# Idle products, halved first weights and row scaling at the hand-over from attention to the first expert

## The chip, the cores and the metric

The kernel runs on one core of a Trainium2 chip. The metric is the device time of one execution in microseconds (us). An engine executes its own instructions in the order in which they were issued to it, and instructions of different engines wait for one another through semaphores. TensorE (PE in the profile; its weight loads are PEld), VectorE (DVE), ScalarE (ACT), GpSimd (POOL) and SyncE (SP, which only issues DMAs here) all take part. The clock of TensorE can be throttled; the profile records the share that was granted.

## The reference

The reference is an attention followed by a mixture of experts whose tokens are assigned by capacity:

```python
scores = scale * np.matmul(q, k.transpose(0, 1, 3, 2))     # q, k, v: 8 x 8 x 576 x 64
thresh = np.max(scores, axis=-1, keepdims=True) - tau
scores = np.where(scores >= thresh, scores, -1000000000.0)
attn = np.exp(scores - np.max(scores, axis=-1, keepdims=True))
attn = attn / (np.sum(attn, axis=-1, keepdims=True) + 1e-09)
x = rows of attn @ v                                       # 4608 x 512
logits = x @ w_gate                                        # 8 experts
order = np.argsort(-logits.flatten())
# walk down the order: a token takes the first expert that still has room, 576 tokens each
for e in range(8):
    out[assigned == e] = np.maximum(x[assigned == e] @ w1[e], 0.0) @ w2[e]
```

w1 is 8 x 512 x 1024, w2 is 8 x 1024 x 512, all in float32.

## The kernel before, in words

**Attention** (`attention`, lines 23 to 356) takes 32 pairs of heads in turn. At its end the last batches are transposed back to rows: `xt_unit` (line 204) does four transposes into PSUM (line 208), two copies on ScalarE (line 218) and a DMA into the DRAM table `xrows` (line 219). A row there has 512 values that are not yet normalised and 8 factors, one for each head. These units stand in the list `late` and are issued between the steps of the first expert search (lines 351 to 355).

**Router.** The experts are filled one after the other. `Router.phase` (line 598) finds an expert's threshold by a search of seven steps: a comparison on VectorE (`step_cmp`), a count by matmuls (`step_cnt`, line 463), a flag (`step_flag`, line 469, whose result `jka` VectorE reads from PSUM), and sums (`step_n`, lines 485 to 499). `pick` names the expert, `rank1` and `rank2` (lines 541 and 542) give each of its tokens a place, and `pack` (line 632) turns the places into a list `idx` of 576 rows: a one-hot compare, matmuls (line 568), a gather by matmuls (line 575) and `compact2`. The first search runs while attention ends (`alone`); the search of expert r+1 runs while expert r is computed. All of them write small results into one PSUM bank: in attention a slot of `sc`, later the single tile `rps`. `warm(n)` (line 594) issues n products of two constant matrices into other columns of that bank; nothing reads them. `pack` of the first expert calls it three times, with 20, 4 and 50 (`WARM`, line 650).

**Experts** (`moe`, line 653). For each expert r:

- `w1_load` (line 675) reads the number of the expert and loads w1 in four tiles `w1s` of 128 x 1024, for expert 0 from ScalarE's queue. Each float32 matrix is split into a rounded high part (`w1h`, a copy on ScalarE) and a low part (`w1l`, a subtraction on VectorE), so that a product is done as three: high x high, high x low, low x high. For expert 0 the four high parts are issued first, then the low parts in column blocks 0, 1, 2 to 3 and 4 to 7, each behind a certain point of `rows`.
- `w2_load` (line 706) does the same for w2 (`w2s`, `w2h`, `w2l`), loaded from SP's queue once GpSimd has copied the number of the expert behind its gathers. The splitting starts once all of w1 is split.
- `rows` (line 723) gathers the 576 rows in five tiles `xg` (four of 128, one of 64) by indirect DMAs from GpSimd (line 729). A tile is scaled by its factors (`scale` on VectorE, or `scale_act`, eight copies of 64 columns on ScalarE, line 739), transposed (`turn`, line 755), copied as the high part `xh` (line 756) and subtracted for the low part `xl` (`low`).
- `ffn` (line 784) does the products. The first layer (line 810) goes over eight blocks f of 128 columns of w1 and two halves of the rows; expert 0 does the first half of the rows (columns 0 to 255) for blocks 0 and 1 first. A block's result passes through ScalarE (relu and the high part of `H`), and VectorE makes the low part of `H`. The second layer (line 842) takes five tiles of rows, with w2 in eight parts.

**What sets the order.** The program is issued in an order that a clock written by hand decides: `clk` counts time, each job is a generator that yields how long its next step should come later, and `ffn` advances the clock by a stated cost for each product (0.25 for a half block of expert 0, 0.132 otherwise, 0.227 in the second layer; line 811, 843). `V.wait()` and `V.ease()` are estimates of when VectorE will be free. A job may wait for a name in the set `done`: `("w1",0)`, `("half",0)`, `("row",0,t)`, `("x",0)`, `"ahead"`. Low parts that can wait are put into `fills` and issued in the gaps of a search, when VectorE is thought free, when they are old, or when `ffn` wants them (`want`). For expert 0, `rows` also issues the start of expert 1's search by hand: `phase` up to its first comparison behind the gathers (lines 740 to 742), then the count and the flag at line 767; the rest runs once `"ahead"` is set. The products start to be issued once `("w1",0)` and `("half",0)` are there. The clock decides the order in each engine's queue, not when an instruction runs.

Of the kernel before, what the change touches and what calls it, by code (L numbers as in the profile page):

```python
# [398 lines left out]
class Router:  # L399
# [198 lines left out]
    def phase(s,last=False):  # L598

        s.stage="search"; V=s.V  # L600
        def held(t): s.pe=t; V.after(V.now+t+0.2)
        if s.first: s.prep(33)
        else:
            yield V.ease()
            s.prep()
            yield V.ease()
        s.alone=s.first; s.first=False
        if last:

            lo=s.wk.tile([128,1],F32,name="lo"); V.memset(lo,-FMAX/4); E={"lo":lo}  # L610
        else:
            E={"E":s.k("E1"),"lv":-1}
            def gap():

                w=V.wait(); s.fill()
                return w
            s.on=True
            for i in range(7):
                s.step_cmp(E); yield gap()
                held(0.34); s.step_cnt(); yield gap()  # L620
                held(0.16); s.step_flag(E["lv"]); yield gap()
                held(0.1); E=s.step_n(E)
                if not s.alone: yield V.ease()
            s.on=False
        s.pick(E)
        if last:
            yield V.wait()
            held(0.13); s.pick2()
        s.stage="pick"; s.rank1(E)
        yield V.wait()  # L630
        held(0.2); s.rank2()
# [16 lines left out]

LATS=[0.15,0.35,0.7]+[0.8]*5; FIX=(0.125,0.15)
GA=[5.0,6.5,8.0,8.0]; AGE=7.0; HALF=1; WARM=[20,4,50]  # L650
W1Y=5.0; L2O=(0,4,1,2,3); L2Z=1; HFB=3; RW=[0.2,0.4,0.4,0.4]; LOWP=(); LPF=7; LOWT=1.4; PREPW=1; WLY=(1.0,1.0)

def moe(ctx,tc,R,start,xrows,w1,w2,out,ident):
    nc=tc.nc
# [20 lines left out]
    def w1_load(r,s):  # L675
# [2 lines left out]
        s["e"]=q.value_load(s["ei"][0:1,0:1],min_val=0,max_val=E-1)  # L678
        for k in range(4):
            t=w1p.tile([128,F],F32,name="w1s",bufs=4); s["w1s",k]=t  # L680
            q.dma_start(t,w1[ds(s["e"],1),k*128:(k+1)*128,:].rearrange("o p f -> p (o f)"))
        yield W1Y if r==0 else 5.0
        while r>0 and ("l1",r-1) not in done: yield 0.5
        s["w1h"]=w1p.tile([128,4,F],F32R,name="w1h"); s["w1l"]=w1p.tile([128,4,F],F32R,name="w1l")
        if r==0:
            for k in range(4):
                A.activation(s["w1h"][:,k],s["w1s",k],AF.Copy); yield 1.1
            done.add(("w1",0))
            for a,b in ((0,1),(1,2),(2,4),(4,8)):
                while (("row",0,1),"scaled",("row",0,4))[min(a,2)] not in done: yield 0.1  # L690
                o=slice(128*a,128*b)
                for k in range(4):
                    V.tensor_tensor(s["w1l"][:,k,o],s["w1s",k][:,o],s["w1h"][:,k,o].bitcast(F32),op=ALU.subtract)
                    if a>1: yield 0.9 if a<4 else 2.0
                for f in range(a,b): done.add(("w1l",f))
            done.add(("w1a",0))
            return
        def lowpart(k,o): V.tensor_tensor(s["w1l"][:,k,o],s["w1s",k][:,o],s["w1h"][:,k,o].bitcast(F32),op=ALU.subtract)
# [7 lines left out]
    def w2_load(r,s):  # L706
        while ("g",r) not in done or (r>0 and ("w2",r-1) not in done): yield 0.5
        e=nc.sync.value_load(s["ei2"][0:1,0:1],min_val=0,max_val=E-1)
        for k in range(4):
            t=wk.tile([128,2,D],F32,name="w2s",bufs=4); s["w2s",k]=t  # L710
            nc.sync.dma_start(t,w2[ds(e,1),k*256:(k+1)*256,:].rearrange("o (k p) d -> p (o k) d",p=128))
        yield 5.0
        while ("w1a",r) not in done or (r==0 and ("x",0) not in done) or (r>0 and ("l2",r-1) not in done): yield 0.5
        s["w2h"]=wk.tile([128,8,D],F32R,name="w2h"); s["w2l"]=wk.tile([128,8,D],F32R,name="w2l")
        def lowpart(k,c): V.tensor_tensor(s["w2l"][:,2*k+c],s["w2s",k][:,c],s["w2h"][:,2*k+c].bitcast(F32),op=ALU.subtract)
        for k in range(4):
            for c in range(2):
                A.activation(s["w2h"][:,2*k+c],s["w2s",k][:,c],AF.Copy)
                yield WLY[0]
                later(("w2l",r,2*k+c) if 2*k+c<7 else ("w2",r),lambda k=k,c=c: lowpart(k,c))  # L720
                yield WLY[1]

    def rows(r,s):
# [8 lines left out]
        def scale(t):  # L732
# [1 line left out]
            n=128 if t<4 else 64  # L734
            v=s["xg",t][:n,:D].rearrange("p (h d) -> p h d",h=8)
            V.tensor_tensor(v,v,s["xg",t][:n,D:XW].unsqueeze(2).to_broadcast([n,8,64]),op=ALU.mult)
        def scale_act(t):
            x=s["xg",t]
            for h in range(8): A.activation(x[:,64*h:64*h+64],x[:,64*h:64*h+64],AF.Copy,scale=x[:,D+h:D+h+1])
        if r==0:  # L740
            step0=R.phase(); R.ahead=step0
            for _ in range(3): next(step0)
        yield GA[min(r,3)]
        while r>0 and ("l1",r-1) not in done: yield 0.5
        s["xh"]=wk.tile([128,4,576],F32R,name="xh"); s["xl"]=wk.tile([128,4,576],F32R,name="xl")
# [16 lines left out]
        if r==0:  # L762


            def step(n=1):
                for _ in range(n): next(R.ahead)
            step(); scale(0); step(); turn(0); scale(1); low(0); turn(1); scale_act(2); yield V.ease()
            low(1); yield 0.25
            scale(3); scale(4); done.add("scaled"); yield 1.8
            turn(2); yield 0.6  # L770
            turn(3); low(2); yield 0.6
            turn(4); low(3); yield 0.6
            low(4); done.add("ahead")
            done.add(("x",0)); return
        scale(order[0]); yield V.wait()
        for i,t in enumerate(order):
# [203 lines left out]
```

## Time and profile before

| | us |
|---|---|
| median of the timed runs (3) | 994.23 |
| lowest and highest of them | 993.36 and 996.37 |
| profiled execution, its own time | 986.18 |
| span of its instructions | 984.40 |
| PE busy | 952.5 |
| DVE busy | 780.3 |
| ACT busy | 633.9 |
| POOL busy | 261.0 |
| mean granted TensorE clock | 0.99 |

The span runs from the first to the last instruction of the profiled execution. A row of a timeline has the start, the length, the engine, the line, the operation, the tile that is written and the tiles that are read, how often (x), and in brackets the idle time of the engine before it with what ended it. Many VectorE instructions have line 395, since a helper issues them; the tiles tell them apart. Ends of PE instructions are modelled, and matmuls overlap. Attention takes the first 460 us, the first search lies between 465 and 486 us, expert 0 starts near 500 us, and the seven others follow, the second at 570 us.

### The profile page before, as it was taken

How to read it: one execution, taken by the hardware profiler on the slowest of the kernel's cores; microseconds unless marked ns; L12 is line 12 of the kernel's file. 1: busy time of each engine (PE TensorE's matmuls, PEld its weight loads, DVE VectorE, ACT ScalarE, POOL GpSimd, SP SyncE). 2: the span in 40 equal slices, each digit the busy share in tenths (PEclk: the TensorE clock that was granted, in tenths of full speed). 3: DMA queues.
4: the chain of work that ended last, by engine and by line, in shares of the span. 5: the costliest groups of instructions: out<-in, count | busy, mean ns of one | idle time of the engine just before them, and what ended most of it. 6: DMA issues, size and time to landing. Idle time of an engine off the chain costs nothing.

```text
span 984.4 us, 24025 instructions
## 1 busy us (share of the span) xinstructions
PE 952.5 (97%) x9140; PEld 708.2 (72%) x9140; DVE 780.3 (79%) x2145; ACT 633.9 (64%) x1256; POOL 261.0 (27%) x419
## 2 busy tenths in 40 slices
PE   6999999999999999999789999999999999999996
PEld 4566665666566556565579798897988979898995
DVE  7999999999999999996679878687787786535220
ACT  6899989899998999997545354353452535445340
POOL 2333433334333333331020412222403113310202
PEclk9999999999999999999979999999999999999998
DMA  6232244144523233304761615242523435341101
GB/s 254 98 107 101 73 154 162 75 143 155 186 100 122 98 122 92 116 2 158 253 201 39 220 41 181 69 151 97 162 103 124 135 111 164 112 141 39 38 11 43
DMA packets 35858, 116.98 MB, mean 119 GB/s; under 512 B 4384, under 2 KB 5024, under 8 KB 35232
## 3 DMA queue, kind: packets, MB, share of 16 engines
q1 hardware_dynamic: 28352, 92.85, 27.6%
q0 software_dynamic: 5888, 19.03, 6.2%
q10 hardware_dynamic: 1504, 3.59, 1.2%
q8 instruction: 72, 1.18, 0.5%
q14 instruction: 42, 0.34, 0.1%
HBM read 93.01 MB, written 21.38 MB: 116 GB/s over the span
## 4 chain that ended last, share of the span: by engine, by line
PE 84%; DVE 7%; ACT 3%; issue 3%; DMA 3%; POOLq 0%; SPq 0%; DVEq 0%; ACTq 0%
PE pf L810 21%; PE pf L842 19%; PE sc L69 13%; PE xo L155 12%; PE tb L98 8%; PE pt L755 2%; PE xo L165 2%; DVE z L74 2%; DVE pp L90 1%; PE xo L208 1%; ACT pp L86 1%; PE rps L463 1%; PE xo L177 1%; PE sc L98 1%; DVE cmp L395 1%
## 5 line engine op out<-in xcount | busy, mean ns | idle before, releaser
L75 POOL TENSOR_SCALAR nb<-nb,taub 128x1 f32<-128x1 f32 x288 | 147.6, 512 | 284.0 <-DVE z L74 242.6
L86 ACT ACTIVATE pp<-z,nb 128x576 f32<-128x576 f32 x256 | 193.3, 773 | 43.1 <-DVE z L74 38.8
L74 DVE TENSOR_SCALAR_CACHE_REDUCE z<-sc 128x576 f32<-128x576 f32 x288 | 205.4, 749 | 9.0 <-PE sc L69 7.5
L90 DVE SCALAR_TENSOR_TENSOR pp<-z,nb,pp 128x576 f32<-128x576 f32 x256 | 199.7, 812 | 0.3
L842 PE MATMUL pf<-w2h,H 128*128 128x512 f32 x576 | 194.8, 402 | 1.3 <-DVE H L395 1.3
L69 PE MATMUL sc<-qk 64*128 64x288 f32 (+1 forms) x1280 | 178.6, 422 | 4.1 <-DVE z L74 1.7
L155 PE MATMUL xo<-pt,vt 128*64 128x320 f32 (+1 forms) x1024 | 155.9, 420 | 0.0
L116 ACT ACTIVATE pt<-tb 128x512 f32<-128x512 f32 x253 | 137.7, 590 | 0.9
L842 PE MATMUL pf<-w2l,H 128*128 128x512 f32 x320 | 128.7, 402 | 0.0
L849 POOL DMA_INDIRECT out_dram<-y,idx x40 | 45.9, 1147 | 310.9 <-ACT y L845 272.5
L842 PEld LDWEIGHTS pf<-w2h,H 128*128 128x128 f32 x576 | 106.5, 189 | 21.0 <-DVE H L395 2.5
L69 PEld LDWEIGHTS sc<-qk 64*128 64x128 f32 (+1 forms) x1280 | 93.4, 178 | 31.7 <-DVE z L74 5.9
L98 PEld LDWEIGHTS tb<-ident,pp 64*128 64x128 f32 x2032 | 74.5, 139 | 57.2 <-issue 26.3
L810 PE MATMUL pf<-xh,w1h 128*128 128x288 f32 (+2 forms) x512 | 110.0, 300 | 0.7 <-ACT xh L756 0.7
L810 PE MATMUL pf<-xl,w1h 128*128 128x288 f32 (+2 forms) x512 | 110.4, 301 | 0.0
L810 PE MATMUL pf<-xh,w1l 128*128 128x288 f32 (+2 forms) x512 | 109.7, 300 | 0.0
L845 ACT ACTIVATE y<-pf 128x512 f32<-128x512 f32 x40 | 23.9, 597 | 129.2 <-PE pf L842 126.2
L155 PEld LDWEIGHTS xo<-pt,vt 128*64 128x64 f32 x1024 | 60.6, 136 | 58.5 <-issue 32.4
L98 PE MATMUL tb<-ident,pp 64*128 64x64 f32 x2032 | 93.3, 229 | 3.3 <-ACT pt L116 3.0
L822 ACT ACTIVATE hf<-pf 128x576 f32<-128x576 f32 x56 | 36.5, 651 | 88.9 <-PE pf L810 87.0
L810 PEld LDWEIGHTS pf<-xh,w1h 128*128 128x128 f32 x512 | 82.2, 190 | 1.6 <-ACT xh L756 1.1
L810 PEld LDWEIGHTS pf<-xl,w1h 128*128 128x128 f32 x512 | 81.9, 190 | 0.1
(199 smaller groups left out, 1324.5 us busy)
## 6 DMA issues: line engine op xcount, KB each, us to landing
qk<-qk_dram SPq DMA_DIRECT2D x31, 864.0 KB, 4.8
vt<-vl_dram SPq DMA_DIRECT2D x32, 576.0 KB, 4.1
w2s<-w_dram SPq DMA_DIRECT2D x32, 512.0 KB, 4.7
w1s<-w_dram SPq DMA_DIRECT2D x28, 512.0 KB, 5.6
xrows<-pp SPq DMA_DIRECT2D x24, 260.0 KB, 2.5
xts<-xt SPq DMA_DIRECT2D x2, 1152.0 KB, 4.7
pt<-xts SPq DMA_DIRECT2D x2, 1152.0 KB, 6.9
xrows<-xr SPq DMA_DIRECT2D x8, 260.0 KB, 2.2
```

The lines of the kernel that those rows point to most:

```text
L69: T.matmul(sc[o,f,:HS], kd["q",h][r,c], kd["k",h][r,:],start=True,stop=True)
L74: V.tensor_scalar(z,SC.pop(t)[:,:,:HS],-0.125,None,op0=ALU.mult,op1=ALU.min,accum_out=nb[:,0:1])
L75: G.tensor_scalar(nb[:,1:2],nb[:,0:1],taub[:,0:1],None,op0=ALU.add)
L86: A.activation(pview(t),ZB[t].rearrange("p a b -> p (a b)"),AF.Exp,bias=NBI[t][:,0:1],scale=-1.0)
L90: V.scalar_tensor_tensor(pv,ZB.pop(t).rearrange("p a b -> p (a b)"),NBI[t][:,1:2],pv,op0=ALU.is_le,op1=ALU.mult,accum_out=den_of(p)[:,i//2 ...
L98: g=slice(64*r,64*r+64); T.transpose(o[:,r],x[r%len(x)][g],ident[g,g])
L116: else: A.activation(o,tb,AF.Copy)
L155: T.matmul(xo[64*h:64*h+64,:q.stop-q.start],v[:,f,128*u+64*h:128*u+64*h+64],PT[p][:,h,u,q],start=new,stop=last,skip_group_check=True)
L810: T.matmul(ps[:,h,:n],s[w][:,k,f*128:(f+1)*128],s[x][:,k,cols[h]],start=(i==0),stop=(i==11))
L822: A.activation(hf,ps[:,:,:HS],AF.Relu)
L842: T.matmul(ps[:,0,:],H[:,f,c:c+128],s[w][:,f],start=(f==0 and j==0),stop=e)
L849: G.indirect_dma_start(out=out,out_offset=IOA(ap=s["idx"][:n,t:t+1],axis=0),in_=y[:n],in_offset=None)
```

## The change

`phase`, when it runs alone, issues 24 idle products between `pick` and `rank1`. The first expert's w1 is loaded in two halves of columns: the first (blocks 0 to 3) from ScalarE's queue as before, the second from SP's queue, in `w2_load`, ahead of the four loads of w2. Its high parts are made in the same halves, the second after the low parts of blocks 2 and 3 and after a mark `"w1x"`, which is set 5.0 + 7.0 of the issue clock after the loads. The low parts of blocks 0 and 1 are issued by `rows`, the first ahead of the first row scaling, the second ahead of the second. VectorE scales all five row tiles, and `scale_act` is gone. `rows` calls `warm` three times: 20 products behind the first comparison of expert 1's search, 20 in front of the first `turn` and 10 in front of the second. The stated delays between the tiles change too.

```diff
@@ phase
         if last:
             yield V.wait()
             held(0.13); s.pick2()
+        if s.alone: s.warm(24)
         s.stage="pick"; s.rank1(E)
         yield V.wait()
         held(0.2); s.rank2()
@@
-W1Y=5.0; L2O=(0,4,1,2,3); ...
+W1Y=1.0; W1X=7.0; L2O=(0,4,1,2,3); ...
@@ w1_load
         for k in range(4):
             t=w1p.tile([128,F],F32,name="w1s",bufs=4); s["w1s",k]=t
-            q.dma_start(t,w1[ds(s["e"],1),k*128:(k+1)*128,:].rearrange("o p f -> p (o f)"))
+            c=slice(0,F//2 if r==0 else F)
+            q.dma_start(t[:,c],w1[ds(s["e"],1),k*128:(k+1)*128,c].rearrange("o p f -> p (o f)"))
         yield W1Y if r==0 else 5.0
@@
         if r==0:
-            for k in range(4):
-                A.activation(s["w1h"][:,k],s["w1s",k],AF.Copy); yield 1.1
-            done.add(("w1",0))
-            for a,b in ((0,1),(1,2),(2,4),(4,8)):
-                while (("row",0,1),"scaled",("row",0,4))[min(a,2)] not in done: yield 0.1
+            def high(c,d):
+                for k in range(4):
+                    A.activation(s["w1h"][:,k,c],s["w1s",k][:,c],AF.Copy); yield d
+            def lows(a,b,d=0.0):
                 o=slice(128*a,128*b)
                 for k in range(4):
                     V.tensor_tensor(s["w1l"][:,k,o],s["w1s",k][:,o],s["w1h"][:,k,o].bitcast(F32),op=ALU.subtract)
-                    if a>1: yield 0.9 if a<4 else 2.0
+                    if d: yield d
                 for f in range(a,b): done.add(("w1l",f))
+            s["lows"]=lambda f: list(lows(f,f+1))
+            yield from high(slice(0,F//2),0.6)
+            done.add(("w1",0))
+            while ("row",0,4) not in done: yield 0.1
+            yield from lows(2,4,0.9)
+            while "w1x" not in done: yield 0.1
+            yield from high(slice(F//2,F),0.8)
+            yield from lows(4,8,2.0)
             done.add(("w1a",0))
             return
@@ w2_load
         e=nc.sync.value_load(s["ei2"][0:1,0:1],min_val=0,max_val=E-1)
+        if r==0:
+            c=slice(F//2,F)
+            for k in range(4): nc.sync.dma_start(s["w1s",k][:,c],w1[ds(e,1),k*128:(k+1)*128,c].rearrange("o p f -> p (o f)"))
@@
         yield 5.0
+        if r==0: yield W1X; done.add("w1x")
@@ rows
         if r==0:
             step0=R.phase(); R.ahead=step0
             for _ in range(3): next(step0)
+            R.warm(20)
         yield GA[min(r,3)]
@@
-            step(); scale(0); step(); turn(0); scale(1); low(0); turn(1); scale_act(2); yield V.ease()
-            low(1); yield 0.25
-            scale(3); scale(4); done.add("scaled"); yield 1.8
-            turn(2); yield 0.6
-            turn(3); low(2); yield 0.6
-            turn(4); low(3); yield 0.6
-            low(4); done.add("ahead")
+            while ("w1",0) not in done: yield 0.1
+            step(); s["lows"](0); scale(0); step(); R.warm(20); turn(0); s["lows"](1); scale(1); low(0); R.warm(10); turn(1); scale(2); low(1)
+            yield 1.3
+            turn(2); scale(3); low(2); yield 3.0
+            turn(3); scale(4); low(3); yield 1.2
+            turn(4); low(4); done.add("ahead")
             done.add(("x",0)); return
```

More of the change, by code (lines that the diff above doesn't have):

```diff
@@ L650 @@
 GA=[5.0,6.5,8.0,8.0]; AGE=7.0; HALF=1; WARM=[20,4,50]
-W1Y=5.0; L2O=(0,4,1,2,3); L2Z=1; HFB=3; RW=[0.2,0.4,0.4,0.4]; LOWP=(); LPF=7; LOWT=1.4; PREPW=1; WLY=(1.0,1.0)
+W1Y=1.0; W1X=7.0; L2O=(0,4,1,2,3); L2Z=1; HFB=3; RW=[0.2,0.4,0.4,0.4]; LOWP=(); LPF=7; LOWT=1.4; PREPW=1; WLY=(1.0,1.0)
 def moe(ctx,tc,R,start,xrows,w1,w2,out,ident):
@@ L736, in scale @@
             V.tensor_tensor(v,v,s["xg",t][:n,D:XW].unsqueeze(2).to_broadcast([n,8,64]),op=ALU.mult)
-        def scale_act(t):
-            x=s["xg",t]
-            for h in range(8): A.activation(x[:,64*h:64*h+64],x[:,64*h:64*h+64],AF.Copy,scale=x[:,D+h:D+h+1])
         if r==0:
```

## The prediction

> **What bounds the kernel now.** I read the page first, then the stretch in which attention hands over to expert 0, then what follows it. A page rows: busy time, share and count of each engine; then the chain that ended last.
>
> ```profile
> PE 952.5 (97%) x9140; PEld 708.2 (72%) x9140; DVE 780.3 (79%) x2145; ACT 633.9 (64%) x1256; POOL 261.0 (27%) x419
> PE 84%; DVE 7%; ACT 3%; issue 3%; DMA 3%; POOLq 0%; SPq 0%; DVEq 0%; ACTq 0%
> ```
>
> TensorE is the bound, so an edit around the hand-over is worth only the time that TensorE idles or runs slowly there. The second view is the table of stretches, cut at 490.00 us and every 3.41 us from there (columns: length, busy us and instructions of PE, PEld, DVE, ACT, POOL, granted clock, DMA share, GB/s).
>
> ```profile
> 5.31:8.72 3.41, 1.84 (x14) 0.92 (x10) 2.08 (x5) 1.45 (x2) 0.58 (x2) 1.00 0.99 381
> 466.11:469.52 3.41, 2.28 (x33) 1.81 (x32) 1.88 (x8) 2.19 (x8) 0.00 (x0) 1.00 0.99 340
> 486.59:490.00 3.41, 1.68 (x22) 1.40 (x23) 2.87 (x11) 0.45 (x2) 0.00 (x0) 1.00 0.50 156
> 490.00:493.41 3.41, 2.80 (x45) 2.65 (x45) 2.88 (x11) 0.21 (x1) 0.00 (x0) 0.50 0.80 286
> 493.42:496.82 3.40, 3.40 (x35) 3.40 (x33) 3.26 (x6) 2.18 (x3) 2.05 (x2) 0.50 0.94 323
> 496.83:500.24 3.41, 1.34 (x27) 1.15 (x25) 0.49 (x3) 1.82 (x2) 2.74 (x3) 1.00 0.68 188
> 500.25:503.65 3.40, 2.21 (x9) 1.83 (x10) 2.06 (x6) 1.52 (x4) 1.15 (x2) 0.50 0.59 177
> 503.66:507.06 3.40, 3.40 (x18) 3.40 (x18) 3.28 (x12) 2.17 (x8) 0.00 (x0) 0.50 0.85 268
> 507.07:510.48 3.41, 3.09 (x26) 2.79 (x25) 3.05 (x10) 0.98 (x2) 0.00 (x0) 1.00 0.92 345
> ```
>
> The granted clock changes only at these cuts. At full clock, stretches with 1.68 and 1.34 us of PE work are followed by half clock, those with 1.84 and 2.28 are not: the border lies between 0.49 and 0.54 busy. From half clock only full stretches (3.40) lead back; 2.80 and 2.21 do not. So 13.7 us run at half clock. In the first half of them TensorE mostly runs idle products; the second half is expert 0's start. PE alone, in order of time, from the last transposes of attention:
>
> ```profile
> 485.64 0.63 PE L208 MATMUL xo<-ident,pt 128*64 128x128 f32 x4
> 487.44 0.21 PE L541 MATMUL rps<-gq,trib 128*128 128x72 bf16 x1 [1.17 <-DVE gq L395]
> 487.77 0.19 PE L542 MATMUL rps<-gx,onesb 128*128 128x72 bf16 x1
> 488.36 1.28 PE L597 MATMUL rps<-trib,onesb 128*128 128x128 bf16 x20 [0.39 <-DVE scol L395]
> 490.61 1.36 PE L568 MATMUL cps<-R,poh 128*128 128x80 bf16 x18 [0.98 <-DVE R L395]
> 491.77 0.63 PE L597 MATMUL rps<-trib,onesb 128*128 128x128 bf16 x4
> 492.38 0.58 PE L575 MATMUL cps<-ob,zz 128*128 128x10 bf16 x16
> 492.81 4.85 PE L597 MATMUL rps<-trib,onesb 128*128 128x128 bf16 x50
> 497.50 0.38 PE L463 MATMUL rps<-oh,cmp 128*128 128x32 bf16 x9
> 498.16 0.29 PE L469 MATMUL rps<-cn,eyer 128*32 128x8 f32 x4 [0.28 <-DVE cn L395]
> 500.76 1.94 PE L755 MATMUL pt<-ident,xg 128*128 128x128 f32 x8 [2.31 <-DVE jka L395]
> ```
>
> The idle 2.31 us before 500.76 are the gather of the first rows; the chain of waits has it:
>
> ```profile
> 487.07 2.23 DMA xrows<-pp
> ...
> 494.46 5.32 DMA xg<-xrows,idx
> ```
>
> From 508.53 on PE is full. What counts is therefore when the first half block (12 products of line 810) is through: its last product starts at 508.39, the next block's first at 508.59.
>
> ```profile
> 508.35 0.18 PE L499 MATMUL rps<-fla,onesb 128*128 128x1 bf16 x1
> 508.39 0.36 PE L810 MATMUL pf<-xh,w1l 128*128 128x256 f32 x1
> 508.59 0.64 PE L810 MATMUL pf<-xh,w1h 128*128 128x256 f32 x4
> ```
>
> **The sum is made against the profiled execution**, 986.18 us (span 984.40). The median of the timed runs, 994.23, lies 8.05 us above it; I carry that difference along unexplained. 0.3%, about what a measurement of this kernel can tell from no change, is 2.98 us.
>
> **24 idle products after the search.** An idle product at full clock takes 1.28/20 = 64 ns; of the 50, the last 0.83 us lie behind 496.83 and hold 13, so 37 ran in 4.02 us at half clock, 108 ns each. The 24 are issued with the search's last step, so they stand ahead of the last four L208 transposes: 1.54 us. The last row write starts at 488.61 instead of 487.07, lands at 490.84, and the w1 load, which waits for it, goes 1.54 us later. That is covered if the half-size loads (1 MB instead of 2) are split before 497.8, when the low parts want them. L541 comes behind them at 485.64+1.54+0.63 = 487.8 instead of 487.44, about 0.2 us of delay for the ranks. In return the stretch to 490.00 gains about 1.2 us of PE work (2.9 of 3.41), so the clock holds; the next has about 2.3, like the 2.28 that held. L568 and L575 then run at full clock (at most half of 1.36 and 0.58 saved). I take the index 0.2 us earlier; bounds 0.2 later and 0.8 earlier.
>
> **The gather and the first weights.**
>
> ```profile
> 493.25 0.17 DVE L395 SCALAR_TENSOR_TENSOR idx<-cps,ih 128x5 int32<-128x5 f32 x1
> ...
> 499.96 0.69 DVE L395 TENSOR_TENSOR xg<-xg 128x512 f32<-128x512 f32 x1 [1.85 <-DMA xg<-xrows,idx]
> ...
> 503.97 0.89 DVE L395 TENSOR_TENSOR w1l<-w1s,w1h 128x128 fp32r<-128x128 f32 x4
> ```
>
> The first gather took 5.32 us beside 2 MB of weights. For expert 2 the five gathers took, from issue:
>
> ```profile
> DMA to landing us min/median/max: 3.2/3.5/3.8
> ```
>
> With half the weights, I take 3.5: rows at 497.8 (bound 499.6). Then 50 and the 20 new products at 64 ns run from 492.6 to 497.1, L463 and L469 to 498.1. VectorE takes cn, then the four low parts of block 0 (0.89) to 498.65, then the first scaling (0.69) to 499.35. Of the 1.85 us wait, the low parts fill a part; before, they stood behind it.
>
> **Twenty and ten products ahead of the transposes.** The second 20 write the bank that jka reads. In the rows above, idle products waited for scol (0.39) though the columns differ; so these wait for jka, behind the first scaling, and start at 499.55. They don't fill the gap of 1.45 us from 498.1; they stand on the path. The stretch 496.83 to 500.24 then has about 1.65 us of PE work, the amount that lost the clock before. Likeliest: half clock at 500.24, and since PE is then full, back at 503.65, one stretch earlier than before. Durations from:
>
> ```profile
> 501.88 0.60 ACT L756 ACTIVATE xh<-pt 128x512 fp32r<-128x512 f32 x1 [2.80 <-PE pt L755]
> ```
> ```profile
> 557.95 0.44 PE pt L755 x4
> ```
>
> Eleven products to 500.24, nine at 108 ns to 501.25; four transposes at half clock (1.94/2 = 0.97) to 502.2; xh to 502.85; the ten (1.08) to 503.3; turn(1), mostly at full clock (0.44), to 503.95; its xh to 504.6. VectorE meanwhile: low parts of block 1 and scale(1) to 501.1, low(0) to 503.6, scale(2) (new on VectorE, 0.69, inside its wait) to 504.3, low(1) to 505.3. Products: four from 504.65 (0.64), eight more from 505.35 (1.28) with turn(2) between (0.44): through at 507.07. Turns 3 and 4, done by then before, are still owed: 0.7. So 507.77 against 508.59: **0.8 us gained**. With rows at 499.6 it is 0.1 lost. ScalarE loses its eight scalings (line 739); it was not the last wait.
>
> **Behind the start.** The issue order is written by a clock: a half-block product counts 0.25, others 0.132. Expert 1's search goes on when "ahead" is set, before 0.25+1.8+3x0.6 = 3.85 after the half was ready, now 1.3+3.0+1.2 = 5.5. That is 1.65 later, seven products of 0.16 us: L499 moves 1.1 us back in PE's order. The second w1 half (four copies, 0.8 each) and this 1.65 put the splitting of w2 4.85 later, two to three of its pairs. SP issues four more w1 loads ahead of the w2 loads, some 2 us; the second half is first wanted by block 4 and w2h at 519.4, so both are covered by blocks 0 to 3.
>
> ```profile
> L718 ACT ACTIVATE w2h<-w2s x8: 613/615/617, 519.4 to 531.1; 128x512 fp32r<-128x512 f32 x8
> L395 DVE TENSOR_TENSOR w2l<-w2s,w2h x8: 673/677/683, 522.4 to 535.1; 128x512 fp32r<-128x512 f32 x8
> ```
> ```profile
> 535.55 0.17 PE L485 MATMUL rps<-jka,hb 32*128 32x1 bf16 x1
> ...
> 542.68 0.49 PE L842 MATMUL pf<-w2h,H 128*128 128x512 f32 x1 [0.24 <-DVE H L395]
> ```
>
> The last line matters: 6 us into the second layer PE already waits for VectorE's last low part of H, which stands behind the ranks of expert 1. So VectorE has no slack there, and a later search gives gain back: between nothing and all of 1.1. I take 0.3. Net 0.5: 986.18 - 0.5 = 985.7, which is 993.7 on the scale of the median.
>
> **Rivals.**
> A. The clock never falls. The cuts have no tie to the program, so another run can cut the 1.45 us gap in two. Then the 20 end at 500.83, turn(0) 501.27, turn(1) 502.35, low(1) 504.05, the half block 505.82, with the owed turns 506.52: 2.1 gained, 0.6 given back, 992.7. For it: 1.65 is close to the 1.84 that held. Against: the row with 1.68. The Trainium skill ("TensorE: Matmul & The Clock Gate", section "Why this matters for your kernels") asks only for no idle gaps over about 3 us, and by that rule A is certain. By that rule the trace disagrees: the longest gap before the fall at 490.00 was 1.17 us. The same page ("Part 4: PE-mode transpose") says that transposes don't count as busy in the same way; by that the clock would come back only at 507.07 and the front would lose about 0.9. The next row disagrees, 1.79 of the 3.40 us that brought the clock back being transposes.
>
> ```profile
> 503.66:507.06 3.40, 1.79 (x8) 1.60 (x8) 0.50 0.85 268
> ```
>
> B. Slower. VectorE becomes the bound in the second layer. Place: the wait at 542.68. Price: 1.65 of the issue clock is 12.5 full-block products of 0.16 = 2.0 us of later search, and three w2 low parts (0.677 each) move behind it, 2.0; of 4.0 the front has gained 0.8: 3.2 slower, 997.4. It decides if these parts and the ranks are issued ahead of H's last low part; for it, the 0.24 that is there already. Against: fewer fillers make the search's steps shorter.
>
> C. The idle products don't do what they are for: the clock falls at 490.00 all the same. Then 70 products end near 498.9, the scaling at 501.2; but PE is busy to 499.3, so the clock holds after 500.24, and the half block with the owed turns is through at 508.3. No change: 994.2.
>
> **Numbers.** Forecast 0.47, A 0.25, B 0.15, C 0.13. Faster than 991.25 is none of the centres; A is 1.45 away: a third of A, and 0.06 of the others, 0.14. Slower than 997.21: three fifths of B, and 0.04 of the others (rows at 499.6, all given back), 0.13. Within: 0.73. The range runs from A with the lowest run's distance from the median (0.9) and half of its give-back undone, some 991.0, to the near edge of B, 997.0.
>
> **What would show it.** In the new profile: 24 idle products ahead of the last L208; last row write 1.5 us later; clock 1.00 through 490 to 500; the first gather shorter than 5.32; the second 20 products right behind jka and not before the scaling; at most one stretch at half clock after 500; first L810 near 504.6, twelve through near 507; the wait at L842 near 542 in the second layer, 0.24 before, at most 1.3. I am wrong if the 20 run before the scaling (then the gap closes and A holds), if the w1 copies are the last wait, or if the second layer waits over 2 us for VectorE.

## The result and the profile after

The changed kernel takes 1000.48 us (median of 12 runs, 996.74 to 1002.16) against 994.4 beside it (12 runs, 993.22 to 998.15): a ratio of 1.0047, with a 95% interval of 1.0035 to 1.0059. It is slower, by about 5 us by the ratio and 6 by the medians, and outside the range that was given. The profiled execution took 1000.57 us (span 998.7).

The page after, its busy row and its chain:

```profile
PE 960.9 (96%) x9214; PEld 713.2 (71%) x9214; DVE 781.0 (78%) x2146; ACT 633.2 (63%) x1252; POOL 259.7 (26%) x419
PE 83%; DVE 7%; issue 3%; ACT 3%; DMA 2%; another core or an unknown queue 0%; POOLq 0%; SPq 0%; DVEq 0%; ACTq 0%
```

PE is busy 8.4 us longer; the 74 idle products, at 64 ns each, account for 4.7 of them. First the hand-over, PE alone in order of time (everything stands 2.51 us later than before, since this execution lost time in attention, where the clock was at half from 41.97 for 3.41 us; the search's last step, L492, started at 488.05 instead of 485.54):

```profile
488.05 0.18 PE L492 MATMUL sc<-jka,onesb 32*128 32x9 bf16 x1
488.16 1.51 PE L597 MATMUL sc<-trib,onesb 128*128 128x128 bf16 x24
489.51 0.60 PE L208 MATMUL xo<-ident,pt 128*64 128x128 f32 x4
...
494.89 4.07 PE L597 MATMUL rps<-trib,onesb 128*128 128x128 bf16 x70
...
501.72 1.37 PE L597 MATMUL rps<-trib,onesb 128*128 128x128 bf16 x20 [1.77 <-DVE jka L395]
502.88 1.06 PE L766 MATMUL pt<-ident,xg 128*128 128x128 f32 x4
503.74 1.27 PE L597 MATMUL rps<-trib,onesb 128*128 128x128 bf16 x10
504.80 1.06 PE L766 MATMUL pt<-ident,xg 128*128 128x128 f32 x4
506.55 0.74 PE L820 MATMUL pf<-xh,w1h 128*128 128x256 f32 x4 [0.69 <-ACT xh L767]
```

And the stretches of 3.41 us at the cuts of the granted clock (columns as before: length, busy us and instructions of PE, PEld, DVE, ACT, POOL, clock, DMA share, GB/s):

```profile
489.12:492.53 3.41, 2.50 (x36) 2.12 (x34) 2.85 (x11) 0.69 (x2) 0.00 (x0) 1.00 0.44 138
492.53:495.94 3.41, 2.63 (x57) 2.46 (x57) 3.24 (x12) 0.00 (x0) 0.00 (x0) 1.00 0.41 100
499.36:502.77 3.41, 1.36 (x24) 1.29 (x24) 2.97 (x13) 1.09 (x2) 2.50 (x4) 1.00 0.62 172
502.77:506.18 3.41, 3.10 (x23) 2.63 (x19) 1.51 (x3) 0.88 (x2) 1.29 (x2) 0.50 0.51 146
506.18:509.59 3.41, 3.04 (x24) 2.85 (x25) 2.19 (x5) 0.92 (x2) 0.00 (x0) 1.00 0.72 228
```

The clock no longer falls behind the search: at the hand-over, half clock is down from 13.7 to 3.4 us. So the front of the change works. The chain of waits (start, length, what) shows the first gather at 4.31 us, shorter than 5.32:

```profile
493.50 3.06 DMA w1s<-w_dram
496.56 4.31 DMA xg<-xrows,idx
```

The loss is 65 us further on. First the same place before: the last step of expert 1's search (L492), then the start of expert 0's second layer.

```profile
535.59 0.16 PE L492 MATMUL rps<-jka,onesb 32*128 32x9 bf16 x1
...
536.85 0.40 PE L842 MATMUL pf<-w2h,H 128*128 128x512 f32 x1
```

And after: expert 0's second layer, then the first layer of expert 1, from 571.68, then the stretches around it:

```profile
537.11 0.47 PE L852 MATMUL pf<-w2h,H 128*128 128x512 f32 x1
...
541.30 0.16 PE L492 MATMUL rps<-jka,onesb 32*128 32x9 bf16 x1
...
544.29 0.50 PE L852 MATMUL pf<-w2l,H 128*128 128x512 f32 x1 [1.02 <-DVE w2l L395]
```
```profile
571.68 0.29 PE L820 MATMUL pf<-xh,w1h 128*128 128x288 f32 x1
572.50 0.29 PE L469 MATMUL rps<-cn,e 128*32 128x8 f32 x4 [0.53 <-DVE cn L395]
573.10 0.40 PE L820 MATMUL pf<-xl,w1h 128*128 128x288 f32 x1 [0.31 <-DVE xl L395]
...
575.25 0.60 PE L766 MATMUL pt<-ident,xg 128*128 128x128 f32 x4
576.49 0.39 PE L463 MATMUL rps<-oh,cmp 128*128 128x32 bf16 x9 [0.64 <-DVE cmp L395]
577.78 0.35 PE L469 MATMUL rps<-cn,eyer 128*32 128x8 f32 x4 [0.91 <-DVE cn L395]
577.99 0.59 PE L820 MATMUL pf<-xh,w1h 128*128 128x288 f32 x1
578.98 0.61 PE L820 MATMUL pf<-xl,w1h 128*128 128x288 f32 x1 [0.40 <-DVE xl L395]
```
```profile
574.45:577.86 3.41, 1.86 (x23) 1.45 (x22) 3.01 (x6) 2.62 (x6) 1.67 (x1) 1.00 0.02 6
577.86:581.27 3.41, 3.01 (x14) 2.58 (x14) 1.74 (x5) 0.17 (x1) 0.00 (x0) 0.50 0.21 76
581.28:584.69 3.41, 3.41 (x16) 3.38 (x16) 2.17 (x3) 1.95 (x4) 0.00 (x0) 0.50 0.00 0
```

The reader is to see three things. The search of expert 1 ends (L492) 4.2 us behind the start of the second layer, 541.30 against 537.11; before, it ended 1.3 us ahead of it (535.59 against 536.85). So the index, the gathers and the rows of expert 1 come late too: two of its five transposes (L766) stand inside its own first layer, between steps of the next search. VectorE has to work for both, and PE waits for it five times, 2.8 us in all. The stretch with the longest two of them (0.64 and 0.91) holds 1.86 us of PE work, and the next 6.83 us run at half clock. This layer took 37.66 us; before, 28.90, without a wait of PE.

A table over the runs makes the sum (us; the first three columns from the start of the search's last step, L492, each worked out from the profile of that kernel; idle and half clock are counted between the second and the third point):

| profile | first product of expert 0 | 13th product (first half block through) | expert 2's first layer | PE idle | half clock |
|---|---|---|---|---|---|
| before | 17.85 | 23.06 | 146.20 | 0.96 | 0 |
| before (e1) | 17.47 | 22.67 | 147.39 | 2.11 | 0 |
| before (e15) | 17.47 | 22.90 | 147.91 | 2.53 | 0 |
| after | 18.50 | 20.72 | 154.61 | 6.48 | 6.83 |
| after (e13) | 18.59 | 20.81 | 151.45 | 6.06 | 0 |
| after (e18) | 18.45 | 20.66 | 151.00 | 4.74 | 3.41 |

Taking idle time and half of the half clock off, the stretch between the points is 122.2 to 122.6 us before and 123.9 to 124.6 after; of the 1.7 more, about 1.0 are the two groups of transposes still owed (0.60 and, for the tile of 64 rows, 0.44). So the front gains 2.3 and owes 1.0; the waits behind it cost about 4, and the clock, where it falls, 1.7 or 3.4 more. Part of the 6.48 is not the order's: 1.07 and 1.21 us of it are waits for VectorE of the kind told of at the end, which e18 lacks, and e1 and e15 have one of (0.92 and 1.02). Behind the start of expert 2's first layer nothing more is lost: from there to the end of the span e18 takes 351.6 us and the first profile of before 352.7.

### The profile page after: what moved, and what is told of

The parts are those of the page before. It is cut to its first block, busy times and chain, and to the rows that moved or that the text cites. A ratio compares the mean times of both kernels' runs of the same rounds, so it can differ in the third digit from the quotient of the medians.

```text
span 998.7 us, 24179 instructions
## 1 busy us (share of the span) xinstructions
PE 960.9 (96%) x9214; PEld 713.2 (71%) x9214; DVE 781.0 (78%) x2146; ACT 633.2 (63%) x1252; POOL 259.7 (26%) x419
## 4 chain that ended last, share of the span: by engine, by line
PE 83%; DVE 7%; issue 3%; ACT 3%; DMA 2%; another core or an unknown queue 0%; POOLq 0%; SPq 0%; DVEq 0%; ACTq 0%
PE pf L820 21%; PE pf L852 19%; PE sc L69 12%; PE xo L155 12%; PE tb L98 8%; PE xo L165 2%; PE pt L766 2%; DVE z L74 2%; DVE pp L90 1%; PE xo L208 1%; ACT pp L86 1%; PE rps L463 1%; DVE cmp L395 1%; PE xo L177 1%; PE sc L98 1%
## 5 line engine op out<-in xcount | busy, mean ns | idle before, releaser
L69 PE MATMUL sc<-qk 64*128 64x288 f32 (+1 forms) x1280 | 181.2, 427 | 3.4 <-DVE z L74 1.3
```

The costliest lines, as they stand in the source:

```text
L69: T.matmul(sc[o,f,:HS], kd["q",h][r,c], kd["k",h][r,:],start=True,stop=True)
```

## The experiments

Each ratio is against runs of the kernel before on the same chip, where that kernel took 994.2 (e1 to e4), 993.9 (e5 to e8), 987.6 (e9 to e12), 996.5 (e13 to e16) and 985.9 (e17, e18). Absolute times of different groups are therefore not compared. All times are medians, of 12 runs except for e5 (6), e18 (5), e1 and e15 (one each); a ratio is not that of the medians and can differ from it by 0.1%.

**The kernel before, once more** (no edit).

> The kernel before, unchanged, for a second profile of it. All theories: time within 0.3% of 994.4 us. Open: whether the shorter first layers of experts 4 and 5 in the first profile (28.9 and 27.3 us against 31.3 and 29.7 after the change) belong to the kernel or to that execution. If to the kernel, they come out at 28.9 and 27.3 again; if chance, at about 31 and 29.5.

> The kernel before, one look, for the waits of VectorE and the stages on the chip of this call. Near 994: two or more waits of VectorE over 1.5 us ahead of cn or jka between 550 and 780 us and experts 4 and 5's first layers near 31; near 986 to 988: none or one, and 28.9 and 27.3.

They took 994.71 and 993.67, with experts 4 and 5's first layers at 31.20 and 31.14, and 31.04 and 29.77 us. The profile that the prediction was made from has 28.89 and 27.29 there. It is an execution of the kind that the chips with 986 and 988 show, so some of what it has less than the profile after is not the change; the table above has e1 and e15 beside it for that reason.

**The order of issue.** The old line ended in `yield V.ease()`, ahead of `low(1)`: a wait of the issue clock for VectorE's estimated backlog. The change drops it. e2 drops it alone; e3 puts it back in the changed kernel.

```diff
 e2, on the kernel before
-turn(1); scale_act(2); yield V.ease()
+turn(1); scale_act(2)
 e3, on the changed kernel
-turn(1); scale(2); low(1)
-yield 1.3
+turn(1); scale(2); yield V.ease()
+low(1); yield 1.3
```

> The kernel before, with only the one yield of V.ease() taken out that stands ahead of low(1) of the first expert; no idle product, no halved load, the same instructions. Issue-order theory (the products of expert 0 start to be issued before VectorE's estimated backlog is paid off, so the search of expert 1 falls back behind them: its last step stands behind 36.1 us of products instead of 32.2): slower by 4 to 6.5 us, 998.5 to 1001; in the profile the last step of expert 1's search 4 us or more into the second layer, and PE waiting for VectorE in the first 8 us of expert 1's first layer. Rival, idle products on the path: 994.4 within 1.5 us, since there are none. Rival, halved weights and later split of w2: 994.4 within 1.5 us.

> The changed kernel with that one yield of V.ease() put in ahead of low(1), all else as changed. Issue-order theory: the last step of the search stands behind 32.2 us of products, as before; expert 1's first layer takes 29 us, and about 2 us gained at the start remain: 991.5 to 994.5. Rival, idle products on the path: 998 to 1001. Rival, halved weights and later split of w2: 998 to 1001.

e2: 996.09, ratio 1.0017 (0.9996 to 1.0039), runs from 990.65 to 999.88. e3: 996.41, ratio 1.0028 (1.0010 to 1.0046). Neither theory was whole. The order itself did what the theory said. Counted in PE's order, the search's last step stands behind 184 products of expert 0 before, behind 207 after, behind 203 in e2 and behind 184 again in e3. The place is settled too: in every profile without that wait the first layer of expert 1 takes over 33 us (e2 33.45; the changed kernel 37.66, 35.13, 36.68; e5 37.87), in every one with it under 30 (e3 29.45; before 28.90). The price is not: e2's interval just takes in no change, and reaches into that of the whole change. Its profile, of its longest run, has a wait of 0.68 us just ahead of that layer and one of 1.06 in it, and 10.2 us at half clock between the table's two points. And putting the wait back leaves a loss. In e3 the wait has moved to expert 0's second layer:

```profile
544.44 0.50 PE L852 MATMUL pf<-w2l,H 128*128 128x512 f32 x1 [1.70 <-DVE w2l L395]
```

**The idle products.** e4 adds all four groups to the kernel before, e6 only those that lie in gaps, the 24 and the first 20; e5 takes all four out of the changed kernel.

```diff
 e4, on the kernel before (e6: without R.warm(20) and R.warm(10) in the last line)
+if s.alone: s.warm(24)
 for _ in range(3): next(step0)
+R.warm(20)
-step(); scale(0); step(); turn(0); scale(1); low(0); turn(1)
+step(); scale(0); step(); R.warm(20); turn(0); scale(1); low(0); R.warm(10); turn(1)
```

> The kernel before with the idle products alone (24, 20, 20 and 10 at the same places), same order of everything else. Issue-order theory: 994.4 within 1.5 us; the clock at full speed from 490 to 500 and at most one stretch of 3.4 us at half speed after it. Rival, idle products on the path: 4 to 6 us slower.

> The kernel before with the 24 idle products after the search and the 20 behind the 50 alone, without the 20 and the 10 that stand ahead of the row transposes. Theory S (only the 20 and 10 behind jka cost, since nothing else is late for them): 993 to 995, clock at 1.00 from 490 to 497, the first transpose of expert 0's rows 15.0 to 15.8 us after the search's last step instead of 14.4 (the rows land later because the 24 hold up the last row write and so the weights), the first layer of expert 0 starting 18 to 19 after it. Rival P (the 24 cost, since they hold up the last row write and the 2 MB of weights behind it): 996 to 997, as with all four groups.

> The changed kernel with none of the 24+20+20+10 idle products; the order of everything else is unchanged. Theory S (two separate terms: the search of expert 1 late in TensorE's order, worth about 4, and the idle products, worth about 2, of which those behind jka stand on the path): 998.3, between 996.5 and 999.5, with expert 1's first layer still 33 us or longer and the granted clock at 0.5 in one stretch from 490. Theory W (the idle products are the whole loss, and the order costs nothing by itself): 994 to 995.5, first layer of expert 1 near 29.5.

e4: 996.28, ratio 1.0022 (1.0012 to 1.0033). e6: 993.53, 1.0001 (0.9983 to 1.0019). e5: 998.81, 1.0040 (1.0025 to 1.0056). For e4 neither expectation came true: it is 2.1 us over before, where the one allowed 1.5 and the other asked for 4 to 6. The second 20 and the 10 stand on the path, as the prediction said; in e4:

```profile
501.44 2.29 PE L597 MATMUL rps<-trib,onesb 128*128 128x128 bf16 x20 [3.81 <-DVE jka L395]
503.53 1.06 PE L757 MATMUL pt<-ident,xg 128*128 128x128 f32 x4
504.38 1.27 PE L597 MATMUL rps<-trib,onesb 128*128 128x128 bf16 x10
```

2.29 + 1.27 = 3.56 us ahead of expert 0, whose first product comes 21.49 us behind L492 instead of 17.47. Without those two groups it comes at 18.04 (e6) and nothing is lost. In the changed kernel the clock falls at 489.70 again without the products (e5), and the loss stays: the products are not its main cause.

**The wait put back, and the products thinned.**

```diff
 e7: as e3, without R.warm(20) and R.warm(10) ahead of turn(0) and turn(1)
 e8: as e7, without s.warm(24) and the first R.warm(20)
```

> The changed kernel with the wait for VectorE's backlog put back ahead of the low part of tile 1, and without the 20 and the 10 idle products ahead of the transposes (the 24 and the first 20 stay). Theory S: 3 us of idle products leave the path of the run with the wait alone (996.4): 992 to 994.3, the first layer of expert 0 starting 15 to 16.5 after the search's last step (17.4 before, 17.4 with all products). Rival P or a cost of the halved weights and of VectorE's third scaling: 995.5 to 997.

> The same without any new idle product: halved weights, early low parts, VectorE scaling all rows, and the wait put back. Theory S: the shorter gather gains up to 1.5 at the front and the clock falls at 490 as before: 992.5 to 994.5, first layer of expert 1 near 29.5. Rival H (the halved weights and the scalings on VectorE cost by themselves, through the second layer of expert 0, 35.2 us in the run with the wait against 34.05): 995.5 to 997, with the second layer of expert 0 at 35 us.

e7: 995.50, ratio 1.0016 (0.9999 to 1.0032). e8: 997.17, 1.0033 (1.0015 to 1.0050). Theory S fell with both: with the wait back and no product on the path there is still something, though e7's interval just takes in 1. Both have it in expert 0 (first layer 34.87 and 35.42, second 35.55 and 35.57 us; 33.6 and 34.4 in e1). For e7:

```profile
513.20 0.39 PE L463 MATMUL rps<-oh,cmp 128*128 128x32 bf16 x9 [1.23 <-DVE cmp L395]
545.84 0.50 PE L852 MATMUL pf<-w2l,H 128*128 128x512 f32 x1 [1.67 <-DVE w2l L395]
```

The low part of w2 that PE waits for is made late because w2 is split behind the second half of w1, which the change puts 5.0 + 7.0 of the issue clock after the loads. The next runs test that.

**w2 split earlier.**

```diff
 e9, on e7
-W1Y=1.0; W1X=7.0
+W1Y=1.0; W1X=2.0
-yield from high(slice(F//2,F),0.8)
+yield from high(slice(F//2,F),0.4)
 e10 = e16, on e9: yield 1.3, 3.0, 1.2 between the rows -> 0.25, 0.8, 0.6
 e11, on e10: lows(4,8,2.0) -> lows(4,8,1.0)
 e14: e9's edit on e3, that is, with all 74 idle products
```

> The run with the wait put back and only the 24 and the first 20 idle products (995.5, second layer of expert 0 at 35.55 us, with a wait of 1.67 for the last low part of w2), and the second half of w1 and so w2 split earlier: 2.0 instead of 7.0 of the issue clock before the second half's copies, 0.4 instead of 0.8 between them. Theory L (what is left of the loss is the late splitting of w2, behind the second half of w1): the wait in the second layer falls under 0.6, the layer to 34.4, the time to 993.3 to 994.8. Rival V (VectorE has too much to do in the first layer whatever the order; what is brought forward makes other steps late): second layer near 34.5 but first layer of expert 0 over 35.3, time 995 to 996.5.

> The same with the three waits between expert 0's rows at 0.25, 0.8 and 0.6 of the issue clock instead of 1.3, 3.0 and 1.2, so that the search of expert 1 goes on earlier (its last step 3.2 us of products further ahead of the second layer). Theory L: 992 to 994, since the search's waits in the second layer (0.57) and in expert 1's first layer (0.47) go as well. Rival V: rows 2 to 4 are wanted by TensorE before VectorE has scaled them, the first layer of expert 0 is 36 us or longer, time 995.5 to 998.

> The same with the last low parts of w1 spaced by 1.0 instead of 2.0 of the issue clock. Theory L: as the run before it or up to 0.7 less. Rival V: as the run before it or longer, with a longer wait in expert 0's first layer.

> The changed kernel, all 74 idle products in it, with the two corrections of the order alone: the wait for VectorE's backlog ahead of the low part of tile 1, and the splitting of w2 earlier (2.0 and 0.4 in place of 7.0 and 0.8). Theory S: what is left over the kernel before are the 20 and 10 products on the path, 1 to 2 us, less the front's gain of up to 1.5: between 0.5 under and 1.5 over before. Rival P (the products cost 2 or more wherever they stand): 2 to 3 over before.

> The version with the wait back, the 24 and the first 20 products alone, w2 split earlier and expert 0's rows earlier, once more. Theory S: 0.1 to 0.4% under before on any chip (0.17% where before took 987.6). Rival D: no shorter than before where before takes 994.

e9: 985.58, ratio 0.9988 (0.9976 to 0.9999). e10: 985.55, 0.9983 (0.9973 to 0.9993). e11: 985.73, 0.9985 (0.9975 to 0.9995). e14: 997.23, 0.9996 (0.9979 to 1.0013). e16: 995.59, 0.9986 (0.9969 to 1.0004). The wait for w2's low part is gone in e9; a wait of 0.53 for the low part of H is left there (0.24 before):

```profile
542.38 0.73 PE L852 MATMUL pf<-w2h,H 128*128 128x512 f32 x2 [0.53 <-DVE H L395]
```

With both corrections of the order, the changed kernel with every one of its products cannot be told from the kernel before (e14), and without the 30 on the path it is 0.1 to 0.2% faster where before takes 987.6; where before takes 996.5 the interval of e16 just takes in 1. On that chip the changed kernel itself (e13, below) has 1.0020: its runs are 2.1 us longer than e14's in the mean, at the edge of what 12 runs of each can tell, and 3.3 longer than e16's. In e14's profile expert 1's first layer is at 29.63, but PE is idle for 6.49 us between the table's points all the same; 4.7 of them are three waits for cn (0.98, 1.07, 2.63), where VectorE stood still or was in a scaling of 2.39 us. The absolute times that were expected for e9 to e11 were wrong by the chip; the ratios are those of theory L.

**VectorE scales the third tile**, alone, in the kernel before.

```diff
-turn(1); scale_act(2); yield V.ease()
+turn(1); scale(2); yield V.ease()
```

> The kernel before with one edit: VectorE scales the third tile of expert 0's rows (0.69 us) in place of ScalarE's eight scalings. The prediction's view (that part lies inside a wait of VectorE and is covered): 994.2, between 993.3 and 995.2. Rival V (each 0.7 us more on VectorE ahead of the first layer comes out at TensorE): 995 to 996, with expert 0's first layer 0.7 longer than 33.6.

985.69, ratio 0.9984 (0.9973 to 0.9996): not slower, against rival V, and about as much faster as e9 to e11 are. Whether these owe their lead to more than this one edit was not separated.

**The changed kernel again, and its waits filled.** e13 and e18 are the changed kernel; e17 adds idle products ahead of the search's steps that wait in expert 1's first layer.

```diff
 e17, on the changed kernel, in phase, for the search of expert 2 (np==3)
+if np==3 and i==3: s.warm(10)
 held(0.34); s.step_cnt(); yield gap()
+if np==3 and i in (2,3): s.warm((8,14)[i-2])
 held(0.16); s.step_flag(E["lv"]); yield gap()
```

> The changed kernel once more, beside the others of this call. The kernel before took 994 in two calls and 987.6 in the third; its waits of VectorE of 1.5 to 3.5 us ahead of cn and jka behind 550 us are there in the executions near 994 and missing in the ones near 986. Theory S (the order costs by itself): 4 to 6 over before whatever before takes here, expert 1's first layer 33 us or longer. Rival D (the order costs only together with those waits): if before takes 986 to 988 here, at most 2 over it, first layer of expert 1 under 32.

> The changed kernel with 8, 10 and 14 more idle products straight ahead of the three steps of the search at which TensorE waits in expert 1's first layer (0.53, 0.64 and 0.91 us in the changed kernel); nothing else is moved. Theory G (the late search costs twice: some 3 us of waits, and in part of the executions 3.4 us more, since the granted clock falls to 0.5 for 6.8 us in the stretch that the waits leave at 0.55 busy): the waits are filled, the clock holds at 1.00 in expert 1's first layer in every execution, so the executions over 999 are gone; median 995.5 to 997.8 where the changed kernel beside it takes 998 to 1000.5, and its profile has a first layer of 34.5 to 36. Rival (the executions over 999 come from elsewhere, waits of VectorE on the chip): the same spread as the changed kernel beside it, with the products' 2 us or less on top.

> The changed kernel as it is, beside the run with filled waits. Theory G: two groups of times, near 995 to 998 and near 999 to 1003, and one profile that has either 35 us without half clock or 37.7 with it in expert 1's first layer, by its group. Rival: one group.

e13: 998.09, ratio 1.0020 (1.0001 to 1.0040), runs from 994.99 to 1003.38. e18: 990.48, 1.0036 (1.0023 to 1.0049), runs from 989.88 to 991.19. e17: 989.36, 1.0030 (1.0020 to 1.0041), from 987.11 to 992.08. Rival D fell with e18: on the chip where before takes 985.9 the change costs 3.5 us by the ratio and 4.6 by the medians, and expert 1's first layer takes 36.68. e13's own 1.6 to 2.0 us are less than the 4 to 6 that theory S wanted, though its profile has the waits in full. The stretches of e13's profile, its lowest run, show the same waits without the fall:

```profile
568.35:571.76 3.41, 2.56 (x17) 1.98 (x18) 3.32 (x9) 1.15 (x3) 0.93 (x1) 1.00 0.08 24
571.76:575.18 3.42, 2.23 (x24) 1.81 (x22) 2.57 (x4) 2.63 (x6) 1.47 (x1) 1.00 0.14 29
575.18:578.59 3.41, 2.38 (x19) 2.09 (x20) 2.48 (x9) 0.60 (x2) 0.00 (x0) 1.00 0.24 82
```

The cuts spread PE's 3 us of waits over three stretches, and the clock holds: the layer takes 35.13 us. In the profile after they leave 1.86 in one stretch (37.66, two stretches at half clock), in e18's 1.19 (36.68, one):

```profile
573.13:576.55 3.42, 1.19 (x17) 0.74 (x16) 3.42 (x9) 2.15 (x4) 1.30 (x1) 1.00 0.22 80
576.55:579.96 3.41, 3.41 (x15) 3.26 (x16) 1.50 (x3) 0.37 (x1) 0.00 (x0) 0.50 0.00 1
```

So the place of the cuts decides up to 3.4 us; that this alone makes the spread of the changed kernel's times (in the first measurement 996.74 to 997.51 in four runs and 1000.37 to 1002.16 in eight) is likely, but not shown. For it speaks the mean granted clock of each run: 0.994 in the mean of the four, 0.990 of the eight, and 0.4% of 1000 us is 4 us where the two groups lie 3.8 apart. Where the clock fell in those runs is not on record. e17 was to show it and doesn't: 1.1 us less than e18 with overlapping times, where theory G wanted 2 to 3. In its profile, of its lowest run, the clock holds up to 978.7 us, and expert 1's first layer takes 35.14. The same profile says why the filling was poor. Two of the three groups themselves wait for VectorE, in the bank that cn is read from:

```profile
567.29 0.61 PE L597 MATMUL rps<-trib,onesb 128*128 128x128 bf16 x8 [0.54 <-DVE cn L395]
572.57 0.94 PE L597 MATMUL rps<-trib,onesb 128*128 128x128 bf16 x14 [0.91 <-DVE cn L395]
```

## Why the prediction was wrong

**The front was right, step by step.** The 24 products stand ahead of the last L208 and cost it 1.5 us; the clock holds behind the search; the second 20 start right behind jka, at 501.72 - 2.51 = 499.21 on the time scale of before (forecast 499.55); one stretch at half clock follows, and it leads back at once. The gather took 4.31 where 3.5 was taken. Half clock lasted from 500.26 to 503.67 on that scale (forecast 500.24 to 503.65); expert 0's first product came at 504.04 (forecast 504.65), and the 13th, behind the half block, at 506.26 (forecast 507.07 for the end of the 12th). Against 0.8 forecast, the front gains 2.3 less 1.0 of owed transposes: 1.3, or 0.9 if e1 is taken for before. That half clock came out within 0.02 us is luck: the cuts happened to lie at the same place of the program in both executions. Rivals A and C did not happen in the profile after. A did in e17, which is the same kernel up to there: the clock never fell, and the 13th product came at 19.44 behind L492 instead of 20.72. That is 1.3 earlier, as much as A's front (2.1) had over the forecast's (0.8).

**The step that failed is "Behind the start".** It took the delay of expert 1's search as the difference of the stated yields, 1.65 of the issue clock, "seven products of 0.16 us: L499 moves 1.1 us back in PE's order". For the search's first step that holds: in PE's order L499 stands behind 19 of expert 0's products, 11 before, eight later where seven were forecast. But the last step (L492) stands behind 207, 184 before: 23 later, eight at the end of the first layer and 15 in the second. The search does not go by stated yields alone: between its steps it yields `V.wait()` and `V.ease()`, which wait until VectorE's estimated backlog is worked off. The change takes a `V.ease()` out of the rows, so that `ffn` begins to issue products while that backlog is still owed, and brings eight low parts and a scaling ahead into it. The steps of the search then wait for it while products pass; the dropped `V.ease()` alone makes 19 of the 23 (e2), and putting it back takes all 23 away (e3). The prediction read the diff's numbers and not its missing yield. The give-back was put at 0.3; the runs show about 4 us of waits, and up to 3.4 of clock. The sign that was named for it, a wait of at most 1.3 near 542 in the second layer, came true (1.02 at 544.29): it looked one layer too early.

**Rival B had the kind of cause, but not the place.** It gave 4.0 for a late search and a late w2 together, 997.4, with 0.15. That its 4.0 came near the waits measured is partly luck, since its late search was the same 1.65 of the issue clock, 12.5 products instead of 23. A wait at the second layer, which it named, exists (1.02 for w2's low part in the profile after; before, 0.24 for H's), and e9 and e14 show that the late splitting of w2 makes it: with it earlier, the waits for w2's low part of 1.67 (e7) and 1.70 (e3) are gone, and 0.53 and 0.52 for H's are left. The larger part came one layer later, in expert 1's first layer, through the rows of expert 1. What it lacked was the clock: a wait of a few us that falls into one stretch costs that stretch's clock as well.

**Two smaller sums of the prediction** don't come out, without bearing on the result: L541 at 487.8 instead of 487.44 is 0.4 us of delay rather than 0.2, and the lower end of the range adds up to 991.5 (992.7 - 0.9 - 0.3) rather than 991.0.

**The idle products** were put on the path rightly but priced only inside the front's sum. Alone they cost 0.22% (e4). The 24 and the first 20 cost nothing (e6); that they gain something in the changed kernel (e7 against e8, 1.0016 against 1.0033) is within the intervals.

The page "TensorE: Matmul & The Clock Gate" of the Trainium skill ("Why this matters for your kernels") asks for no idle gap over about 3 us. The trace disagrees again: the longest gap in the stretch ahead of 577.86 was 0.91 us, and the clock fell.

## What to carry to other kernels

When an issue order is made by a clock with estimates in it, a removed yield is a change like any other: list for each job what it waits for, and compare the order of the instructions of both kernels on the bound engine, to the last step of each job and not only to the first. When a front is tightened, follow the work that used to hide in its slack (here the next search and the splitting of w2) to the place where the bound engine next waits for it. Idle products that fill a gap cost nothing here (e6), though no run shows that they gain time either; they cost their full time where the buffer that they write makes them wait for the very step that ends the gap (e4).

## What the runs showed of the hardware

- **The share of busy time in a stretch does not give the border of the clock.** Stretches with 1.84 (before, 5.31 to 8.72), 2.23 and 2.38 us of PE work (e13) were followed by full clock, those with 1.36 and 1.86 (after) by half clock. In e3 one with 1.71 (541.91 to 545.32) was followed by full clock, in e2 one with 2.19 by half clock. So the border that the prediction put between 0.49 and 0.54 busy is none:

```profile
575.83:579.24 3.41, 2.19 (x24) 1.64 (x24) 2.90 (x5) 2.20 (x5) 1.84 (x1) 1.00 0.20 77
579.25:582.66 3.41, 3.41 (x17) 3.26 (x16) 1.76 (x5) 0.59 (x1) 0.00 (x0) 0.50 0.00 0
```

- **The way back is not all of a stretch.** After half clock with 3.10 us of PE work (502.77 to 506.18) came full clock, after 3.01 (577.86 to 581.27) it did not; in e4 2.72 (503.83 to 507.24) led back, in e16 a full 3.41 (557.48 to 560.89) did not. The prediction had taken it that only 3.40 leads back.

- **Some chips have waits of VectorE that nothing in the trace explains.** On those where the kernel before takes 993.9 or more, VectorE stands still for 1.5 to 3.6 us ahead of the small instructions of the search, though PE's result is there. In e1 the count (L463) is through at 768.10, and VectorE takes it 3 us later; PE loses 2.11. First VectorE, then PE:

```profile
767.55 0.69 DVE L395 TENSOR_TENSOR w2l<-w2s,w2h 128x512 fp32r<-128x512 f32 x1
771.13 0.19 DVE L395 CAST cn<-rps 128x32 fp32r<-128x32 f32 x1 [2.89 <-remote]
```
```profile
767.71 0.39 PE L463 MATMUL rps<-oh,cmp 128*128 128x32 bf16 x9
771.37 0.29 PE L469 MATMUL rps<-cn,e 128*32 128x8 f32 x4 [2.11 <-DVE cn L395]
```

e1 has three such waits over 1.5 us behind 490 us (counted from the end of the product that VectorE waits for), e15 four, and each of the twelve profiles e1 to e8 and e13 to e16 two to five. The first profile of before has none, and neither have the six on the chips where before takes 985.9 and 987.6 (waits of 1.9 in e17 and e18 end with PE's own result). They explain part of the 8 us between the profiled execution of before and the median of its runs. One trait they share: GpSimd is issuing indirect DMAs, gathers or writes of rows, during all 43 that the twelve profiles and the profile after have. But the first profile of before has the same gathers without such a wait, so what causes them stays open.
